# Splitting the products from scores and states around second-layer products in four of seven blocks

## The chip, the cores and the metric

The kernel runs on one core of a Trainium2 chip. The metric is the device time of one execution in microseconds (us), as the median of several runs. The core has TensorE (PE, matrix products; PEld is its loading of weights), VectorE (DVE), ScalarE (ACT), GpSimd (POOL) and SyncE (SP, which issues most DMAs). Each engine works through its own list of instructions in order, and waits for others by semaphores.

## The reference

An attention block of the RWKV-6 kind feeds a two-layer network. There are 4 sequences of 768 tokens, 8 heads of 48 columns; the network has 384 inputs, 2048 hidden columns and 384 outputs, all in 32-bit floats.

```python
for t in range(S):
    cur = np.einsum('bhd,bhe->bhde', u[None] * kt, vt)
    y[:, :, t] = np.einsum('bhd,bhde->bhe', rt, state + cur)
    state = wt[:, :, :, None] * state + np.einsum('bhd,bhe->bhde', kt, vt)
...
h = x @ w_in          # x is y, turned to (tokens, heads * columns)
g = h - np.tanh(h)
out = g @ w_out
```

## The kernel before

**Blocks and units.** The 3072 tokens are taken in 8 blocks of 384 tokens, two for each sequence (`q` is 0 for the first half and 1 for the second). The main loop `for i, blk in enumerate(blocks)` runs the network for block `i`, in 16 units `f`, each of 128 hidden columns. Within it, the attention of the next block (`later`, block `i + 1`) is made bit by bit in the units, so that its result `xT` is ready when block `i + 1` begins. What follows counts blocks by `i`, the block whose network runs; `later.q` is then 1 for even `i` and 0 for odd `i`. Block 7 has no later block, so there are seven phases of each kind.

**A unit.** TensorE first makes the first layer (`first`, line 870: three matmuls into the PSUM tile `hp`, each with 384 columns). ScalarE and VectorE turn `hp` into `g` (lines 873 to 902). Then come the second-layer products that are due: `due` is a list of (time, function, operands), and `add_due(now)` issues those whose time has come, some units after their `g`. In block 0 a unit's second layer is three matmuls of 384 columns (`Second.add`, line 947). In the later blocks a scheme with fewer products is used: VectorE forms sums of pieces of `g` and of the weights (`form_g`, line 917; `form_w`, line 1240), and a unit has six products of 128 columns (`Fewer.add`, line 994), into the PSUM tiles `acc`. A matmul of 32-bit floats stands twice in the profile, each time with a load of weights, so line 870 has six records in a unit, line 947 six, line 994 twelve.

**The attention of the next block.** In chunks of 64 tokens. `own` or `diagonal_in` and `earlier` make the scores within a chunk (tile `scores`, which the code calls `A`; VectorE writes them at lines 396 and 501). `update_1` and `update_2` make the state at each chunk's start: TensorE at line 574, VectorE at line 586 (tiles `states0`, `states1`). The function `plan(i)` has written out by hand in which unit each phase is issued: `results`, the last of them, stands in unit 13 for `i` of 0 and 1 and in unit 12 for the others.

**The results phase.** `Block.together` takes two PSUM tiles (`att0`, `att1`) for the result and adds two products into them for each head and chunk: scores times values, and the decayed `r` (tile `pre`) times the state. All its matmuls stand at line 756. Their operands are small (64 or 48 rows by 48 columns, 64 columns moved). They go in four stretches of 24 products (48 records): scores with `cross` 0, scores with `cross` 1, states with `cross` 0, states with `cross` 1. For a first half of a sequence (`later.q` of 0) the very first chunk has no state, so the states have 80 records instead of 96. Within one `cross` the second stretch adds onto the first, so it begins behind a tiny GpSimd memset (`ended_at`, line 763) that waits for the first stretch's last matmul. After the last stretch, ScalarE copies the result out (`result_out`, line 728, four copies) and SyncE moves the columns that lie elsewhere (`fill_holes`, line 776, six small DMAs).

**Order around it.** In the loop over units the phases other than `results` are issued first, then the DMA loads, then `add_due(now)`, and only then `later.together(ps_a)` (line 1362). So TensorE's list reads: first layer of the unit, second-layer products that are due, scores, states, first layer of the next unit.

Of the kernel before, what the change touches and what calls it, by code (L numbers as in the profile page):

```python
# [63 lines left out]
ALL = tuple(range(NPAIR))  # L64
# [12 lines left out]
UNITS = [(0, 0), (0, 1)] + [u for j in range(NF // 2 - 2) for u in ((1, j), (0, j + 2))] + [(1, NF // 2 - 2),  # L77
                                                                                      (1, NF // 2 - 1)]
LATE = 3

# [43 lines left out]
def kernel(  # L126
# [12 lines left out]
    nc = tc.nc  # L139
# [46 lines left out]
    def draw(names, cols):  # L186
        nc.gpsimd.memset(mask_all[0:L, cols], 1.0)
        for m in names:
# [5 lines left out]
            else:  # L194
# [13 lines left out]
    states = [states0[:, 0:NPAIR * NCH * L].rearrange("d (p c e) -> d p c e", c=NCH, e=L),  # L208
              const.tile([P, NPAIR, NCH, L], F32, name="states1", tag="states1")]
# [13 lines left out]
    def g_at(q, x):  # L223
        if not isinstance(x, str):
# [9 lines left out]
    n_whole = blocks_n * NPAIR * NCH  # L234
    light = [n for n in range(blocks_n * NF) if NF - LATE <= n < blocks_n * NF - 2 and
             (n < NF or few[n // NF])]
# [76 lines left out]
    def begin_behind(ins, then):  # L313
        tc.add_manual_dep(then.ins, ins.ins.name, mybir.DependencyInfo(
            mybir.DependencyClass.Sync, mybir.DependencyReason.DATA))
# [3 lines left out]
    class Block:  # L319
# [408 lines left out]
                    copies.append((copy[h] if copy else nc.scalar.copy)(out=dst[rows], in_=src[rows]))  # L728
            return copies[0]

        def together(self, ps):

            self.results(ps)
            yp, spread, St, ended = self.yp, isinstance(ps, Kept), states[self.q], {}

            def scores(p, c, h, par):
                toks = slice(64 * par, 64 * par + 64)
                return self.v[toks, c, p * D2 + h * D:p * D2 + (h + 1) * D], A[toks, h, p, c, :]

            def from_state(p, c, h, par):  # L740
                rows = slice(64 * h, 64 * h + D)
                return St[rows, p, 2 * c + par, 0:D], self.chunk("pre", p, 2 * c + par, spread)[rows]

            def stretch(of, cross):
                first = cross not in ended
                begun = set()
                for n in range(UP):
                    for c in range(NCP):
                        for h in range(2):
                            for x in range(2):  # L750
                                p, par = UP * n + x, x ^ cross
                                if of is from_state and not (self.q or c or par):
                                    continue
                                lhs, rhs = of(p, c, h, par)
                                e0, n0 = 64 * (h ^ x), (n * NCP + c) * L
                                done = nc.tensor.matmul(yp[x][e0:e0 + D, par, n0:n0 + L], lhsT=lhs, rhs=rhs,  # L756
                                                        start=first and (x, e0) not in begun, stop=True,
                                                        skip_group_check=True)
                                begun.add((x, e0))
                                if not first and len(begun) == 1:  # L760
                                    begin_behind(ended[cross], done)
                if first:
                    ended[cross] = nc.gpsimd.memset(ended_at, 0.0)
                    begin_behind(done, ended[cross])

            for of in (scores, from_state):
                for cross in range(2):
                    stretch(of, cross)
            self.result_out(ALL)
            self.fill_holes([nc.sync])  # L770

        def fill_holes(self, engines, which=range(2 * KC)):
            for n in reversed(which):
# [68 lines left out]
        def general(self, ps):  # L842
            self.begin()
            self.load_v()
            for name, as_ in (("k", "k"), ("r", "r"), ("k", "post"), ("r", "pre")):
                for p0 in HALVES:
                    self.load(name, p0, UP, as_=as_)
            src = wT[self.b, :, :, self.q * NCH * LP:(self.q + 1) * NCH * LP]
            for p in range(NPAIR):
                nc.sync.dma_start(out=self.tokens("w", p, 1).rearrange("d (c t) -> d c t", t=L),  # L850
                                  in_=src[p].rearrange("d (c j) -> d c j", j=LP)[:, :, 1:])
            for name, odd in (("k", 1), ("r", 0)):
                for p in range(NPAIR):
                    t = self.tokens(name, p, 1).rearrange("d (n two) -> d n two", two=2)[:, :, odd]
                    nc.scalar.activation(out=t, in_=t, func=AF.Copy, scale=u_sb[:, p:p + 1])
            for p0 in HALVES:
                mask = masks[1].rearrange("s b j -> s (b j)")
                self.masked(ps, "k", "r", mask, p0)()
                self.decay(1, p0, UP)
                self.totals(1, p0, UP)  # L860
                for m in (2, 4, 8, 16, 32):
                    self.level(ps, m, p0, UP)
                    self.totals(m, p0, UP)
                self.turn(ps, p0)
                self.update_any(ps, p0, self.tots[L])
            self.together(ps)

    def first(xT, f, hp):
        for kc in reversed(range(KC)):
# [336 lines left out]
    ps_a = Kept(mains.enter_context(tc.tile_pool(name="ps_a", bufs=1, space=PSUM)))  # L1206
# [8 lines left out]
    ahead_of_h, rest, formed, extra, behind, due, summed = [], [], [], [], [], [], []  # L1215
# [26 lines left out]
    for i, blk in enumerate(blocks):  # L1242
        here = xT
        later = blocks[i + 1] if i + 1 < len(blocks) else None
# [7 lines left out]
        for f in range(NF):  # L1252
# [36 lines left out]
            rest, behind, formed, forming, held_back = later_ops, [], [], held_back, []  # L1289
# [33 lines left out]
            for of, names in ((later, before.get(f, ())), (after, ahead.get(f, ()) if i else ())):  # L1323
                for name in names if of else ():
                    if not now:
                        late.append(lambda of=of, name=name: of.prepare(name))
                    elif now < 2 or name.startswith("bound"):
                        of.prepare(name)
                if of is later:
                    for name in phases.get(f, ()) if later else ():  # L1330
                        behind += later.phase(ps_a, name)
            if i == 0 and f == NF - 3:
                early.close()
                wide = ctx.enter_context(tc.tile_pool(name="wide", bufs=1))
# [9 lines left out]
            for name in loads.get(f, ()):  # L1344
                of, ins = (after if name in ("w", "k", "r") else later), None
# [13 lines left out]
                    behind.append(summed[0].others_summed)  # L1359
            add_due(now)  # L1360
            if later and "results" in phases.get(f, ()):
                later.together(ps_a)
        if fewer and later:
            summed.append(fewer)
    sum_held(ends[:, 1:3], top[:, n_top - 2:], ends, count)
# [14 lines left out]
    with tc.If(anew > 0, label="anew"):  # L1380
        with tc.manual_schedule(engines={PE, SP, DVE, ACT}), ExitStack() as again_pools:
            ps_d = again_pools.enter_context(tc.tile_pool(name="ps_e", bufs=1, space=PSUM))
            ps_a = again_pools.enter_context(tc.tile_pool(name="ps_b", bufs=2, space=PSUM))
# [64 lines left out]
```

## Time and profile before

| | us |
|---|---|
| median of 3 runs | 552.23 (550.72 to 553.09) |
| the profiled execution | 552.88, its span 551.1 |
| TensorE busy | 536.8 (97% of the span) |
| VectorE busy | 459.3 (83%) |
| ScalarE busy | 403.6 (73%) |
| line 870, first layer, tile hp | 260.1 |
| line 756, the results phases | starting between 78.8 and 466.9 |

In the views, times are from the span's start. A row of the timeline has the start, the length, engine, line, operation, tiles (out<-in), shapes and the number of instructions merged; in square brackets stands the idle time before it and what ended it ("issue" means that the profile shows nothing that the engine waited for). A row of the list of waits has the total, the number of times and the longest. A row of the view by windows has the window and its length, then for PE, PEld, DVE, ACT and POOL the busy time and the number of instructions, then the granted clock of TensorE, the DMA share and GB/s. A row of the DMA queues has packets, MB and share of time.

### The profile page before, as it was taken

The page shows a single profiled execution, that of the slowest core. Times are in us where ns is not written, and L with a number is a line of the kernel's source. Part 1 is how long each engine was busy: PE and PEld are TensorE (multiplying, and loading weights), DVE is VectorE, ACT ScalarE, POOL GpSimd, SP SyncE. Part 2 cuts the span into 40 slices and gives each one's busy share as a digit, 9 for nine tenths or more (in the row PEclk, how much of TensorE's full clock was granted, in tenths as well). Part 3 has the DMA queues.
Part 4 walks back from the last instruction along what each step waited for, and adds up shares of the span by engine and source line. Part 5 has one row for each costly group of instructions (what it writes and reads, how often), then busy time and mean ns, then how long its engine had stood idle before and what let it go on. Part 6 is the DMA issues. An engine that isn't in the chain of part 4 may idle for free.

```text
span 551.1 us, 14091 instructions
## 1 busy us (share of the span) xinstructions
PE 536.8 (97%) x5682; PEld 404.7 (73%) x5682; DVE 459.3 (83%) x943; ACT 403.6 (73%) x814; POOL 6.5 (1%) x47
## 2 busy tenths in 40 slices
PE   8999989999999999999999999999999999999996
PEld 5756655677777787878777787777877777787874
DVE  7899997899979989799897889879787897557563
ACT  5899975897568886688666887588855986666561
POOL 1100000000000000000000000000000000000000
PEclk9999998999999999999999999999999999999999
DMA  7798632252302532144112532126222320200101
GB/s 273 256 398 320 216 116 70 86 129 75 118 11 87 113 113 92 57 122 138 61 55 50 139 117 66 50 87 160 66 86 63 82 63 2 56 0 1 45 1 46
DMA packets 53045, 56.29 MB, mean 102 GB/s; under 512 B 21488, under 2 KB 50928, under 8 KB 52976
## 3 DMA queue, kind: packets, MB, share of 16 engines
q1 hardware_dynamic: 52592, 55.18, 32.8%
q8 instruction: 45, 0.74, 0.6%
q14 instruction: 24, 0.20, 0.1%
q10 hardware_dynamic: 288, 0.10, 0.1%
q0 software_dynamic: 96, 0.07, 0.1%
HBM read 44.73 MB, written 4.72 MB: 90 GB/s over the span
## 4 chain that ended last, share of the span: by engine, by line
PE 92%; DVE 4%; issue 2%; DMA 1%; SPq 0%; DVEq 0%
PE hp L870 43%; PE acc L994 26%; PE att L994 6%; PE acc L947 5%; PE att L756 4%; PE att L493 2%; PE acc L972 2%; PE att L574 2%; PE att L870 1%; DMA r<-in_rT 1%; PE acc L870 1%; DVE scores L501 1%; DVE first_states L630 0%; DVE pre L416 0%; DVE w_sb L267 0%
## 5 line engine op out<-in xcount | busy, mean ns | idle before, releaser
L870 PE MATMUL hp<-xT,w_sb 128*128 128x384 f32 x738 | 260.1, 489 | 0.0
L870 PEld LDWEIGHTS hp<-xT,w_sb 128*128 128x128 f32 x738 | 132.1, 191 | 69.4 <-issue 0.3
L994 PE MATMUL acc<-forms,g 128*128 128x128 f32 x954 | 133.2, 276 | 0.0
L873 ACT ACTIVATE h<-hp 128x384 f32<-128x384 f32 x123 | 60.2, 489 | 98.8 <-PE hp L870 98.3
L994 PEld LDWEIGHTS acc<-forms,g 128*128 128x128 f32 x954 | 122.0, 192 | 10.3
L876 DVE SCALAR_TENSOR_TENSOR h<-h,s 128x384 f32<-128x384 f32 x128 | 70.6, 551 | 60.4 <-ACT s L891 60.4
L917 DVE TENSOR_TENSOR g<-g 128x256 f32<-128x256 f32 x265 | 103.1, 418 | 7.4 <-PE acc L994 6.5
L892 ACT ACTIVATE qa<-s,shift 128x384 f32<-128x384 f32 x113 | 69.5, 615 | 3.7
L894 ACT ACTIVATE junk<-s,shift 128x384 bf16<-128x384 f32 x113 | 67.7, 599 | 0.0
L876 DVE SCALAR_TENSOR_TENSOR g<-qa,h 128x384 f32<-128x384 f32 x112 | 61.5, 550 | 1.6 <-ACT qa L902 0.2
L891 ACT ACTIVATE s<-h 128x384 f32<-128x384 f32 x113 | 59.1, 523 | 3.6
L994 PEld LDWEIGHTS acc<-w_sb,g 128*128 128x128 f32 x318 | 46.8, 191 | 9.7 <-ACT sums L962 0.3
L994 PE MATMUL acc<-w_sb,g 128*128 128x128 f32 x318 | 53.0, 276 | 0.0
L994 PE MATMUL att<-w_sb,g 128*128 128x128 f32 x212 | 35.5, 275 | 0.0
L994 PEld LDWEIGHTS att<-w_sb,g 128*128 128x128 f32 x212 | 31.1, 192 | 5.3
L947 PE MATMUL acc<-w_sb,sums 128*128 128x384 f32 x96 | 34.6, 498 | 0.2 <-DVE sums L876 0.2
L1029 DVE TENSOR_TENSOR sums<-sums 128x256 f32<-128x256 f32 x84 | 32.7, 405 | 1.7 <-ACT sums L1006 1.4
L263 ACT ACTIVATE up<-raw 128x768 f16<-128x768 f32 (+1 forms) x32 | 32.9, 1061 | 0.0
L947 PEld LDWEIGHTS acc<-w_sb,sums 128*128 128x128 f32 x96 | 18.6, 196 | 13.5 <-DVE sums L876 1.1
L416 DVE TENSOR_TENSOR_SCAN pre<-w,start 128x780 f32<-128x780 f32 x14 | 24.9, 1782 | 0.8
L428 DVE TENSOR_TENSOR_SCAN post<-w,seed 128x780 f32<-128x780 f32 x14 | 24.8, 1775 | 0.0
L894 ACT ACTIVATION_READ_ACCUMULATOR junk<-s,shift 128x1 f32 x113 | 21.1, 187 | 0.0
(118 smaller groups left out, 530.1 us busy)
## 6 DMA issues: line engine op xcount, KB each, us to landing
raw<-in_weights SPq DMA_DIRECT2D x16, 768.0 KB, 6.3
w<-in_wT SPq DMA_DIRECT2D x7, 780.0 KB, 4.5
k<-in_kT SPq DMA_DIRECT2D x7, 768.0 KB, 4.7
r<-in_rT SPq DMA_DIRECT2D x7, 768.0 KB, 4.5
v_sb<-in_v SPq DMA_DIRECT2D x8, 576.0 KB, 4.0
k<-in_tokens SPq DMA_DIRECT2D x7, 576.0 KB, 3.9
r<-in_tokens SPq DMA_DIRECT2D x7, 576.0 KB, 4.7
out_y<-sums SPq DMA_DIRECT2D x18, 128.0 KB, 1.8
```

The costliest lines, as they stand in the source:

```text
L263: return lambda: nc.scalar.activation(out=to, in_=of, func=AF.Copy, scale=scale, bias=bias)
L416: return nc.vector.tensor_tensor_scan(out=self.tile("pre")[:, cols], data0=self.tile("w")[:, cols], data1=start[:, 0:n * NCH * LP], initia ...
L870: nc.tensor.matmul(hp, lhsT=w_in_sb[:, f, kc, :], rhs=xT[kc], start=(kc == KC - 1), stop=(kc == 0))
L873: return h, nc.scalar.activation(out=h, in_=hp, func=AF.Copy, scale=1.0 / UPSCALE)
L876: return lambda: nc.vector.scalar_tensor_tensor(out=out, in0=in0, scalar=scalar, in1=in1, op0=op0, op1=ALU.mult)
L891: nc.scalar.activation(out=s, in_=h, func=AF.Square)
L892: nc.scalar.activation(out=qa, in_=s, func=AF.Square, bias=shift[:, 4:5])
L894: nc.scalar.activation(out=junk[:, 0:NB], in_=s, func=AF.Relu, bias=shift[:, 5:6], accum_out=excess[:, at:at + 1])
L917: return lambda: nc.vector.tensor_tensor(out=G[:, to:to + 2], in0=two(G, g_at(q, a0), g_at(q, a1)), in1=two(G, g_at(q, b0), g_at(q, b1)), ...
L947: nc.tensor.matmul(acc, lhsT=g[:, j * P:(j + 1) * P], rhs=w_out_sb[:, f, :], start=(f == self.first), stop=(f == NF - 1))
L994: nc.tensor.matmul(to, lhsT=G[:, g_at(q, a), :], rhs=rhs, start=start, stop=stop, skip_group_check=True)
L1029: ops.append(lambda op=op, at=at: nc.vector.tensor_tensor(out=at[0], in0=at[1], in1=at[2], op=OPS[op]))
```

## The change

`together` becomes `products(ps, part)`, with two parts. Part 0 takes the two PSUM tiles and issues the first two stretches, part 1 issues the other two, the copies and the small DMAs. Which product comes first now depends on the half of the sequence: for `q` of 0 scores come first, as before; for `q` of 1 (even `i`) states come first and scores second.

For `i` of 2, 4 and 6 (`JOINED`) both parts are issued where `together` was, after `add_due`. For `i` of 0, 1, 3 and 5 part 0 is issued with the other phases, ahead of `add_due`, and part 1 behind it, so that TensorE's list reads: first layer, two stretches, second-layer products, two stretches, first layer of the next unit. The GpSimd memsets between a stretch and the one that adds onto it stay, and no drain of TensorE is put in.

```diff
+JOINED = 2, 4, 6
...
-        def together(self, ps):
-
-            self.results(ps)
-            yp, spread, St, ended = self.yp, isinstance(ps, Kept), states[self.q], {}
+        def products(self, ps, part):
+
+            if not part:
+                self.results(ps)
+                self.ended = {}
+            yp, spread, St, ended = self.yp, isinstance(ps, Kept), states[self.q], self.ended
...
-            for of in (scores, from_state):
-                for cross in range(2):
-                    stretch(of, cross)
-            self.result_out(ALL)
-            self.fill_holes([nc.sync])
+            for cross in range(2):
+                stretch((from_state if self.q ^ part else scores), cross)
+            if part:
+                self.result_out(ALL)
+                self.fill_holes([nc.sync])
...
-            self.together(ps)
+            for part in range(2):
+                self.products(ps, part)
...
                     for name in phases.get(f, ()) if later else ():
-                        behind += later.phase(ps_a, name)
+                        if name != "results":
+                            behind += later.phase(ps_a, name)
+                        elif i not in JOINED:
+                            later.products(ps_a, 0)
...
             if later and "results" in phases.get(f, ()):
-                later.together(ps_a)
+                for part in range(i not in JOINED, 2):
+                    later.products(ps_a, part)
```

## The prediction

> **What bounds the kernel now.** I read the page first, then the waits of TensorE alone, then the timeline of TensorE around each of the seven products phases (line 756), then the stretches by window.
>
> ```profile
> span 551.1 us, 14091 instructions
> PE 536.8 (97%) x5682; PEld 404.7 (73%) x5682; DVE 459.3 (83%) x943; ACT 403.6 (73%) x814; POOL 6.5 (1%) x47
> q8 instruction: 45, 0.74, 0.6%
> PE 92%; DVE 4%; issue 2%; DMA 1%; SPq 0%; DVEq 0%
> ```
>
> TensorE is busy 97% of the span and is 92% of the chain that ended last; only its idle time and its slow time can be won. The next answer lists what it waited for between 30 and 540 us, after the start and before the end:
>
> ```profile
> PE att L756 <- issue: 4.8, 4, 1.7
> PE att L756 <- DVE scores L396: 1.4, 1, 1.4
> ```
>
> So 6.2 us stand at line 756 (nothing else there is over 0.2), and two kinds must be told apart: one wait for VectorE, and four that the profile can put down to nobody ("issue"). Block 0 has the first and one of the second:
>
> ```profile
> 72.90 2.10 PE L870 MATMUL hp<-xT,w_sb 128*128 128x384 f32 x6
> 75.19 2.20 PE L947 MATMUL acc<-w_sb,sums 128*128 128x384 f32 x6 [0.19 <-DVE sums L876]
> 78.82 1.56 PE L756 MATMUL att<-scores,v_sb 64*48 64x64 f32 x96 [1.43 <-DVE scores L396]
> 80.20 1.41 PE L756 MATMUL att<-pre,states 48*48 48x64 f32 x85
> 83.26 0.42 PE L756 MATMUL att<-pre,states 48*48 48x64 f32 x11 [1.66 <-issue]
> 83.62 3.11 PE L870 MATMUL hp<-xT,w_sb 128*128 128x384 f32 x6
> 89.28 2.10 PE L870 MATMUL hp<-xT,w_sb 128*128 128x384 f32 x6
> 93.16 2.10 PE L870 MATMUL hp<-xT,w_sb 128*128 128x384 f32 x6
> ```
>
> The other three are in blocks 1, 3 and 5; block 2 shows a phase that has none (4 and 6 look like it):
>
> ```profile
> 145.31 0.61 PE L994 MATMUL acc<-w_sb,g 128*128 128x128 f32 x4
> ...
> 146.74 1.56 PE L756 MATMUL att<-scores,v_sb 64*48 64x64 f32 x96
> 148.12 1.07 PE L756 MATMUL att<-pre,states 48*48 48x64 f32 x57
> 150.26 0.59 PE L756 MATMUL att<-pre,states 48*48 48x64 f32 x23 [1.08 <-issue]
> 150.78 2.20 PE L870 MATMUL hp<-xT,w_sb 128*128 128x384 f32 x6
> ...
> 208.64 1.56 PE L756 MATMUL att<-scores,v_sb 64*48 64x64 f32 x96
> 211.47 2.20 PE L870 MATMUL hp<-xT,w_sb 128*128 128x384 f32 x6
> ...
> 272.60 1.56 PE L756 MATMUL att<-scores,v_sb 64*48 64x64 f32 x96
> 273.98 1.34 PE L756 MATMUL att<-pre,states 48*48 48x64 f32 x70
> 276.03 0.42 PE L756 MATMUL att<-pre,states 48*48 48x64 f32 x10 [0.71 <-issue]
> ...
> 401.47 1.56 PE L756 MATMUL att<-scores,v_sb 64*48 64x64 f32 x96
> 402.85 1.23 PE L756 MATMUL att<-pre,states 48*48 48x64 f32 x65
> 405.43 0.44 PE L756 MATMUL att<-pre,states 48*48 48x64 f32 x15 [1.35 <-issue]
> 405.80 2.20 PE L870 MATMUL hp<-xT,w_sb 128*128 128x384 f32 x6
> ```
>
> The stall falls after 85, 57, 70 and 65 of the second type's matmuls, never at a boundary of the code (a stretch is 48 recorded matmuls, since each product of 32-bit floats is recorded twice). What the four places share is their distance. I counted TensorE's recorded instructions from the middle of each stall to the middle of the next:
>
> ```profile
> 81.90:149.80 67.90, 65.93 (x638) 47.31 (x637) 61.67 (x121) 50.49 (x107) 0.58 (x5) 0.97 0.35 97
> 149.80:275.70 125.90, 125.06 (x1403) 98.51 (x1403) 111.20 (x228) 94.67 (x199) 0.64 (x8) 1.00 0.31 87
> 275.70:404.80 129.10, 128.05 (x1403) 100.71 (x1403) 111.17 (x231) 95.95 (x202) 0.64 (x8) 1.00 0.32 90
> ```
>
> 638 + 637 = 1275 and twice 1403 + 1403 = 2806. The queue named "instruction" carries 0.74 MB in 45 packets, 16.4 KB each, and 11,364 matmuls and weight loads over 45 are 253 a packet. If a packet is 256 instructions, the distances are 5 x 256 = 1280 and 11 x 256 = 2816, less a few synchronising instructions that the rows leave out. So I read the stalls as TensorE running out of fetched instructions: a phase issues a matmul and its load every 14.4 ns (1.38 us for 96), and 192 such pairs are 384 instructions in 2.83 us (208.64 to 211.47). How long a refill needs follows from the rows. In block 1 the stall comes 96 + 57 pairs = 306 instructions into the phase, so the boundary before it was passed after 50, at 147.10; work resumes at 150.26, 3.16 us later. The same working gives 2.9 us in block 3, 3.5 in block 5 and 3.7 in block 0. A block of 256 that is run faster than that ends in a wait.
>
> [...]
>
> The last row of interest is the slow time: line 870 took 3.11 us from 83.62 instead of 2.10.
>
> ```profile
> 77.94:81.35 3.41, 2.53 (x179) 2.53 (x182) 3.41 (x5) 0.85 (x3) 0.18 (x2) 1.00 0.66 226
> 81.35:84.76 3.41, 1.75 (x32) 1.13 (x21) 3.28 (x7) 1.04 (x3) 0.00 (x0) 1.00 0.02 5
> 84.76:88.18 3.42, 3.42 (x7) 1.88 (x6) 3.01 (x6) 1.94 (x5) 0.00 (x0) 0.50 0.12 29
> ```
>
> After a stretch with TensorE busy for only 1.75 of 3.41 us, the granted clock was 0.50 for the next 3.42 us. The stretch before it (2.53 busy) was not followed by a drop.
>
> **The change part by part.**
>
> *Block 0, order.* Now: first layer, six second-layer matmuls (line 947), 96 scores, 96 states. After: first layer, states, the six, scores. The one thing that is late there is VectorE's last write of the diagonal into the scores:
>
> ```profile
> 76.86 1.91 DVE L396 COPY_PREDICATED scores<-mask_all,diagonal 128x768 f32<-128x768 uint8 x2
> ```
>
> The states do not read it, and no wait of TensorE for states or their factors stands in the list. The first layer's follower can start 1.94 us after 72.90, at 74.84 (line 870 repeats every 3.88 us with six others between). Then 1.42 for the states (half of 2.83), 1.94 for the six: 78.20. The scores still wait for that write, which ends at 78.77, so they start at 78.82 as now, and the next first layer at 78.82 + 1.42 = 80.24 instead of 83.62: 3.38 us. This contains the refill: the block of 256 that now ends in the stall then holds 122 small pairs (1.76), the six (1.94) and the wait (0.62), 4.3 us against 3.7 needed, so it no longer starves.
>
> *Block 0, clock.* From 83.62 to 89.28 twelve matmuls take 5.66 us instead of 3.88. With the 1.66 us stall gone I take the halving as gone too: 1.78 us. Bounds: nothing, or 1.78. I take 1.78, because the window from 77.94 would have 0.9 us idle at most, as in the row that caused no drop. [...]
>
> *Blocks 1, 3, 5, order.* Twelve second-layer matmuls (line 994, from 145.31 to 146.74, 1.43 us) go from before the scores to between scores and states. The phases take 4.04 us (146.74 to 150.78), 3.78 (the next line 870 starts 0.35 after 276.03) and 4.33 to the next first layer, against 2.83 x 176 / 192 = 2.60 unstarved: 1.44 + 1.18 + 1.73 = 4.35 us at stake. In the new order the starving block holds 116 small pairs (1.67 us), the twelve (1.43) and about 0.17 of switching: 3.27 us, against 3.16, 2.88 and 3.48 needed. So blocks 1 and 3 just pass, and block 5 is 0.2 short and pays about 0.36 to restart. I take back 0.6 us; the bounds are 0 and, if every refill is as slow as 3.7, 3 x 0.8 = 2.4.
>
> *Switching.* A split adds one turn from large to small matmuls and back. Block 2 shows its price: 192 pairs at 14.4 ns are 2.76 of 2.83 us, and the start comes about 0.1 after the last large one: 0.17 a turn, 0.7 for four blocks.
>
> *Waits.* The second half of each phase waits for a GpSimd memset behind the first half. It is now covered by the other stretch (0.7 us); with the second layer between, by more. No engine gets a wait that it had not. Later second-layer products free their operands later: they end at 273.98 in block 3 instead of 272.5, and VectorE's next write of a form starts after that, with 0.6 of cover:
>
> ```profile
> 274.59 0.42 DVE L917 TENSOR_TENSOR g<-g 128x256 f32<-128x256 f32 x1
> ```
>
> If that cover were gone, VectorE would stand for the overlap, up to 1.4 us, not TensorE at once. ScalarE's four copies, SyncE's six small DMAs and the loads keep their places in their queues; they wait for the phase's end, which comes earlier.
>
> *Blocks 2, 4, 6.* Nothing is split, but states come before scores, so TensorE needs the states 1.42 us sooner:
>
> ```profile
> 206.12 0.36 DVE L586 TENSOR_TENSOR states<-states,whole 128x192 f32<-128x192 f32 x1
> 398.57 0.35 DVE L586 TENSOR_TENSOR states<-states,att 128x192 f32<-128x192 f32 x1
> ```
>
> The last update ends at 206.48, 2.16 us ahead of the phase: cost nothing. In block 5 it ends at 398.92; the scores, which overwrite the PSUM that it reads, would start at 400.04: 1.1 us of cover.
>
> *Does VectorE allow it?* TensorE would be 5.2 us early from block 0 on.
>
> ```profile
> 84.90:111.00 26.10, 26.10 (x91) 16.07 (x91) 20.80 (x37) 18.77 (x43) 0.00 (x0) 0.94 0.27 82
> 111.00:146.70 35.70, 35.70 (x383) 27.79 (x381) 34.84 (x74) 29.44 (x61) 0.41 (x3) 1.00 0.46 123
> ```
>
> VectorE idles 26.10 - 20.80 = 5.3 us up to 111 and then only 0.9 until 146.7. It can come forward by just those 5.3 us, and needs to, since later it has no room. I count this as enough, at its limit.
>
> *Sum.* 3.38 + 1.78 + 4.35 - 0.6 - 0.7 = 8.2 us. The profiled execution took 552.88 us (span 551.1), 0.65 over the median of 552.23; from the median the time is 544.0 us.
>
> **The rivals.**
>
> 1. *Refills still starve the odd blocks.* If the fetch is slower once, or starts later, 1.43 us of cover is too little. If each keeps a stall of 0.6 and a restart of 0.36, 4.35 - 2.9 = 1.5 are left there: 5.16 + 1.5 - 0.7 = 6.0, and 546.2. For it: 3.27 against 3.48 in block 5. Against: blocks 1 and 3.
> 2. *The stall belongs to the states, not to the fetch.* Then it moves with them. In block 0: 74.84 + 1.42 + 1.96 + 1.94 = 80.16, scores end 81.58: 2.0 gained, with the clock 3.8; in the odd blocks 0; less switching 0.7: 550.9, or 549.1 with the clock. Against it: blocks 2, 4 and 6 have the same stretches and no stall. [...]
> 3. *VectorE is the true limit.* It follows only halfway and the odd blocks' gain is lost in the same way: some 2.6 us kept, 549.6. For it: 0.9 us of idle in 35.7. Against: TensorE shows no wait for it there.
> 4. *Slower: the clock gate.* If each half of a split phase counted as idle, up to eight windows would run at half rate, 1.78 us each: 14.2 more, while 8.2 are won: 558. It decides from seven windows. Against it: small matmuls filled most of 2.53 busy us without a drop, and so in all other phases.
>
> **How the numbers follow.** About 0.5% (2.8 us) is what a measurement of this kernel can tell from no change. Forecast 0.72, own range 541.5 to 546; rival 1 0.12; rival 2 0.06; rival 3 0.06; rival 4 0.04. Faster: 0.72 + 0.12 + half of rival 3 = 0.87; slower 0.04; same 0.09. The low end is everything at stake without deductions (9.5, 542.7) less about a microsecond, as the runs spread from 550.72 to 553.09. The high end, 549.0, takes in rival 1 and most of rival 3.
>
> **What would show it.** Right: no "issue" wait over 0.5 us at line 756 in any block; in block 0 scores starting at about 78.8 behind six second-layer matmuls and the next first layer at 80.2; granted clock 1.00 from 84.8; TensorE 5 us earlier at the start of block 1 and still at 146. Wrong: "issue" waits left in blocks 1, 3, 5 (rival 1); a stall inside the states before the second layer (2); new waits of TensorE for VectorE between 100 and 150 us (3); clock below 1.00 in a split phase (4).

## The result, and the profile after

The changed kernel took 545.93 us (545.27 to 548.4, six runs), the kernel before 551.12 (550.69 to 553.09, six runs, among them the three of the table above): a ratio of 0.9904, with a 95% interval from 0.9879 to 0.9928. The forecast was 544.0 us, in a range of 541.5 to 549.0. The profiled executions are 552.88 us before and 546.00 after, which is 6.9 us, while the medians differ by 5.2; the difference between these two numbers is explained below.

From the page after, the span, the busy times and the shares of the chain that ended last, and then TensorE's whole list of waits between 30 and 540 us:

```profile
span 544.3 us, 14092 instructions
PE 535.2 (98%) x5682; PEld 403.6 (74%) x5682; DVE 458.9 (84%) x943; ACT 403.7 (74%) x814; POOL 6.6 (1%) x47
...
PE 93%; DVE 3%; DMA 2%; issue 1%; PEld 0%; SPq 0%; PEldq 0%; DVEq 0%
```

```profile
PE att L759 <- DVE scores L397: 0.3, 1, 0.3
```

The work is the same (5682 matmuls); the four waits with no releaser are gone, and of the wait for VectorE 0.3 of 1.4 us are left. Line numbers are a little higher than before: 756 is 759, 870 is 874, 947 is 951, 994 is 998, 493 is 494. TensorE's timeline in block 0:

```profile
73.41 2.10 PE L874 MATMUL hp<-xT,w_sb 128*128 128x384 f32 x6
75.44 1.56 PE L759 MATMUL att<-pre,states 48*48 48x64 f32 x96
76.94 2.20 PE L951 MATMUL acc<-w_sb,sums 128*128 128x384 f32 x6
79.48 1.56 PE L759 MATMUL att<-scores,v_sb 64*48 64x64 f32 x96 [0.34 <-DVE scores L397]
80.97 2.20 PE L874 MATMUL hp<-xT,w_sb 128*128 128x384 f32 x6
83.00 2.10 PE L951 MATMUL acc<-w_sb,sums 128*128 128x384 f32 x6
84.94 2.10 PE L874 MATMUL hp<-xT,w_sb 128*128 128x384 f32 x6
```

This execution was 0.51 us late when it came here (first layer at 73.41, before at 72.90). The next first layer starts at 80.97 and not at 83.62, and takes 2.20 us and not 3.11. The window in which the clock had been halved now shows 1.00 as the granted clock (third number from the end):

```profile
84.76:88.18 3.42, 3.42 (x13) 1.96 (x12) 3.25 (x7) 1.78 (x6) 0.00 (x0) 1.00 0.32 62
```

Blocks 1 and 5 in TensorE's timeline:

```profile
139.03 2.10 PE L874 MATMUL hp<-xT,w_sb 128*128 128x384 f32 x6
141.06 1.56 PE L759 MATMUL att<-scores,v_sb 64*48 64x64 f32 x96
142.54 0.71 PE L998 MATMUL acc<-w_sb,g 128*128 128x128 f32 x4
143.09 1.06 PE L998 MATMUL acc<-forms,g 128*128 128x128 f32 x8
144.08 1.48 PE L759 MATMUL att<-pre,states 48*48 48x64 f32 x80
145.48 1.24 PE L874 MATMUL hp<-xT,w_sb 128*128 128x384 f32 x3
...
392.13 2.10 PE L874 MATMUL hp<-xT,w_sb 128*128 128x384 f32 x6
394.16 1.56 PE L759 MATMUL att<-scores,v_sb 64*48 64x64 f32 x96
...
397.18 1.80 PE L759 MATMUL att<-pre,states 48*48 48x64 f32 x80
398.91 1.56 PE L874 MATMUL hp<-xT,w_sb 128*128 128x384 f32 x4
```

The states of block 5 take 1.80 us where block 1 needs 1.48: a rest of the wait, 0.33 us, is still there. TensorE's lead over the kernel before, read at the first layer behind each phase, grows at just the four split blocks: 2.65 us behind block 0 (83.62 - 80.97), 4.34 once the slow clock of before is past (89.28 - 84.94), 5.30 behind block 1 (150.78 - 145.48), 5.30 behind block 2 (211.47 - 206.17), 5.98 behind block 3 (276.38 - 270.40) and 6.89 behind block 5 (405.80 - 398.91). With the late start of 0.51 taken out, block 0's order gave 3.16, its clock 1.69, and blocks 1, 3 and 5 gave 0.96, 0.68 and 0.91.

VectorE over the same 36 instructions, before and after (line 876, now 880, stands at both ends; the second window cuts a 37th):

```profile
85.11:111.25 26.14, 26.14 (x93) 16.27 (x92) 20.72 (x36) 18.78 (x42) 0.00 (x0) 0.94 0.27 82
```

```profile
85.67:106.91 21.24, 21.24 (x83) 13.55 (x82) 20.36 (x37) 16.32 (x37) 0.00 (x0) 1.00 0.29 96
```

Before, it idled 26.14 - 20.72 = 5.4 us there; now it idles 21.24 - 20.36 = 0.9. It starts the stretch 0.56 us later than before and ends it 4.34 earlier. It came forward with TensorE and had only just the room for it.

### The profile page after: what moved, and what is told of

It reads as the page before. It is cut to its first block, busy times and chain, and to the rows that moved or that the text cites. A ratio compares the mean times of both kernels' runs of the same rounds, so it can differ in the third digit from the quotient of the medians.

```text
span 544.3 us, 14092 instructions
## 1 busy us (share of the span) xinstructions
PE 535.2 (98%) x5682; PEld 403.6 (74%) x5682; DVE 458.9 (84%) x943; ACT 403.7 (74%) x814; POOL 6.6 (1%) x47
## 4 chain that ended last, share of the span: by engine, by line
PE 93%; DVE 3%; DMA 2%; issue 1%; PEld 0%; SPq 0%; PEldq 0%; DVEq 0%
PE hp L874 43%; PE acc L998 27%; PE att L998 7%; PE acc L951 5%; PE att L759 3%; PE att L494 2%; PE acc L976 2%; PE att L575 2%; PE att L874 1%; DMA xT<-late 1%; DMA r<-in_rT 1%; PE acc L874 1%; DVE scores L502 1%; DVE w_sb L268 0%; DVE post L429 0%
```

## The experiments

Theory A: TensorE's list is fetched in blocks of 256 instructions (the prediction's estimate, from 253 recorded matmuls and loads a packet); a phase that runs a block faster than the next one arrives ends in a wait, and the split helps because slow matmuls then lie in that block. Theory B: the wait belongs to the states' stretch. A third view, called a rival in the expectations: the split as such ends the wait, wherever the fetch stands.

The fetch itself stands in the trace of the kernel before. In the window from 147.5 to 150.2 us, up to the end of block 1's wait, the DMA engines began one packet and nothing else, on the queue named "instruction", at 147.88 us (the sixth of the 40 slices of the first row):

```profile
GB/s 0 0 0 0 0 243 0 0 0 0 0 0 0 0 0 0 0 0 0 0 0 0 0 0 0 0 0 0 0 0 0 0 0 0 0 0 0 0 0 0
q8 instruction: 1, 0.02, 2.2%
```

In blocks 0, 1, 3 and 5 such a packet begins at 80.80, 147.88, 273.58 and 402.49 us, takes 0.9 to 1.4, and TensorE goes on 1.4 to 1.6 us after its end. In block 2, whose phase runs from 208.64 to 211.47 us without a wait, one begins at 205.70 and the next only at 211.11.

The first four kernels below ran on one chip, where the kernel before took 551.75 us (17 runs); the changed kernel with a longer list ran beside the two placed ones, with 552.36 for the kernel before (17 runs); the one with half the work between ran beside the one placed later, with 551.49 (11 runs).

**No block split, order alone.** All blocks joined, so that states come before scores in blocks 0, 2, 4, 6 and nothing else changes.

```diff
-JOINED = 2, 4, 6
+JOINED = 0, 1, 2, 3, 4, 5, 6
```

> The changed kernel with no block split: only the order of the two products is changed in blocks 0, 2, 4 and 6 (states first). Theory A, TensorE runs out of fetched instructions at a fixed place of its list: in block 0 an issue wait of 0.8 to 1.7 us now lies in the scores, which come second; blocks 1, 3, 5 keep 1.1, 0.7 and 1.3 us in the states. Time 549 to 550, against 551.1 for the kernel before. Theory B, the wait belongs to the states: in block 0 it lies in the states, which come first, and the scores have none; time about the same.

Measured: 554.35 us, 1.0048 (1.0029 to 1.0067) of the kernel before. Its profiled execution is the fastest of seven, with 550.98. TensorE in block 0:

```profile
78.11 1.56 PE L759 MATMUL att<-pre,states 48*48 48x64 f32 x96
79.73 1.45 PE L759 MATMUL att<-scores,v_sb 64*48 64x64 f32 x85
83.63 0.42 PE L759 MATMUL att<-scores,v_sb 64*48 64x64 f32 x11 [2.46 <-issue]
83.99 2.20 PE L874 MATMUL hp<-xT,w_sb 128*128 128x384 f32 x6
```

The wait stands in the scores now, after 96 + 85 matmuls as before, so it goes by the place in the list and not by the product: theory B falls here. The time was missed. The wait is longer than expected, 2.46 us, and takes back nearly all that the order gained (from the first layer ahead of the phase, at 73.38, to the one behind it 10.61 us, before 72.90 to 83.62, 10.72). The six other runs took 553.1 to 556.0 us, with a mean granted clock of 0.989 to 0.997 against 1.000 in the profiled one; they left no trace, so that their clock fell in block 0 is only argued. In block 0 the order alone gains next to nothing; the split without the order was not run.

**Block 0 alone.**

```diff
-JOINED = 2, 4, 6
+JOINED = 1, 2, 3, 4, 5, 6
```

> Block 0 split, blocks 1, 3 and 5 joined as before. If the two parts of the gain add up (both theories): block 0's 3.2 us are kept and the 2.6 us of the odd blocks are lost, whose issue waits of 1.1, 0.7 and 1.3 us are back: 547.9, 2.4 to 2.6 over the changed kernel. If VectorE and not TensorE sets the time behind block 0, the waits come back without the time.

Measured: 548.47 us, 0.9935 (0.9915 to 0.9955). Its waits of TensorE:

```profile
PE att L759 <- issue: 3.3, 3, 1.1
PE att L759 <- DVE scores L397: 0.3, 1, 0.3
```

As expected: 2.5 us over the changed kernel's 545.93, which another chip gave, and the three waits are back (1.15, 1.12 and 1.06 us). In the profiles, from the first layer behind block 0's phase to the one behind block 6's it takes 384.6 us against 381.9, 2.7 more. The time comes back with them, so VectorE is not the bound behind block 0.

**All seven split.**

```diff
-JOINED = 2, 4, 6
+JOINED = ()
```

> Blocks 2, 4 and 6 split as well. Theory A: their places in the list cause no wait, so a split gives nothing and costs its two turns between large and small matmuls, 0.30 us each as in the profile of the changed kernel: 0.9 us over the changed kernel, 546.8. A rival, that a split is worth something in itself (cover for the GpSimd memset): 1 us or more under it.

Measured: 546.89 us, 1.0 over the changed kernel's 545.93 from the other chip, without any "issue" wait from 30 us on. From the first layer behind one phase to the one behind the next it is 61.02 us in block 2 (145.00 to 206.02) against 60.69 in the changed kernel (145.48 to 206.17); in blocks 4 and 6 64.30 against 63.96. A split of a phase that has no wait costs 0.34 us and gives nothing. The TensorE rows of block 2, split:

```profile
199.48 2.10 PE L874 MATMUL hp<-xT,w_sb 128*128 128x384 f32 x6
201.51 1.56 PE L759 MATMUL att<-pre,states 48*48 48x64 f32 x96
203.00 1.16 PE L998 MATMUL acc<-forms,g 128*128 128x128 f32 x8
...
204.53 1.56 PE L759 MATMUL att<-scores,v_sb 64*48 64x64 f32 x96
206.02 2.20 PE L874 MATMUL hp<-xT,w_sb 128*128 128x384 f32 x6
```

A stretch of 96 that ends in large matmuls takes 1.49 us to the first of them (201.51 to 203.00), one that is followed by its like 1.38 (78.82 to 80.20 before). What the 0.11 us are, no run shows.

**The kernel before, with a longer list.** 120 instructions more, all in the start.

```diff
-        own = blk.own(ps, h1, spare=94, ahead=5, late=6)
+        own = blk.own(ps, h1, spare=157, ahead=5, late=3)
```

> The kernel before, with TensorE's list made 120 instructions longer during the start (63 more of the small filler matmuls, 3 fewer of the long ones, about 0.3 us in sum), nothing else. Theory A: the issue waits leave blocks 0, 1, 3 and 5 and stand in blocks 2, 4 and 6 instead, 1.1 to 1.7 us each; block 0 keeps its wait of 1.4 us for VectorE; no halved clock from 84 us on; time 549 to 550.5. Theory B: the waits stay in blocks 0, 1, 3 and 5 with their lengths, and the time is 551.4.

Measured: 552.55 us, 1.0016 (0.9995 to 1.0037). Its waits of TensorE, and its timeline in blocks 1 and 2:

```profile
PE att L756 <- issue: 3.5, 3, 1.2
PE att L756 <- DVE scores L396: 1.4, 1, 1.4
```

```profile
146.27 1.56 PE L756 MATMUL att<-scores,v_sb 64*48 64x64 f32 x96
147.65 1.46 PE L756 MATMUL att<-pre,states 48*48 48x64 f32 x80
149.04 2.20 PE L870 MATMUL hp<-xT,w_sb 128*128 128x384 f32 x6
...
206.89 1.56 PE L756 MATMUL att<-scores,v_sb 64*48 64x64 f32 x96
208.27 1.52 PE L756 MATMUL att<-pre,states 48*48 48x64 f32 x92
210.84 0.32 PE L756 MATMUL att<-pre,states 48*48 48x64 f32 x4 [1.05 <-issue]
211.08 2.20 PE L870 MATMUL hp<-xT,w_sb 128*128 128x384 f32 x6
```

The waits changed places as theory A says: 1.05, 1.21 and 1.24 us in blocks 2, 4 and 6, none in 0, 1, 3 and 5; each again ends 1.2 to 1.4 us after an instruction packet has landed. The time was missed by 2 us: the start itself has a dense part, and a refill of 1.31 us now fell there (at 19.3 us), with a halved clock from 21.3 to 24.7. Two numbers are of use later. Block 1's phase, unsplit and unstarved, takes 149.04 - 146.27 = 2.77 us. And block 0, which kept its wait of 1.44 us for VectorE but not the refill, shows no halved clock.

**The changed kernel, with a longer list.** The same edit of the start, made to the changed kernel.

> The changed kernel with the list 120 instructions longer, as in the shifted kernel before. Theory A: the split blocks 0, 1, 3, 5 have no wait wherever the refill falls, the joined blocks 2, 4, 6 now have one each of 1.0 to 1.3 us (with restart 4 to 4.5 in sum), and the start is 1 to 3 us longer as it was there: 550 to 553. So the choice of blocks holds for one length of the list only.

Measured: 551.6 us, 0.9983 (0.9955 to 1.0012). The profile has three "issue" waits at the products' line, 1.16, 1.19 and 1.11 us, all in the joined blocks 2, 4 and 6:

```profile
PE att L759 <- issue: 3.5, 3, 1.2
```

At this length blocks 0, 1, 3 and 5 have no "issue" wait in the kernel before either (the run above), so the run does not test their splits; it shows the joined ones starving. The choice of blocks 2, 4 and 6 holds for one length of the list only: 120 instructions more in the start, and the gain is gone. Of the 5.75 us over the changed kernel beside it (545.85), 4.4 lie in the blocks by the profiles (385.9 us from behind block 0's phase to behind block 6's, against 381.6 in that kernel's profile there), and the rest ahead of them.

**Half the work between.** In blocks 1, 3 and 5 three of the six products go ahead of the scores, three stay between.

```diff
                         elif i not in JOINED:
+                            if i:
+                                _, add, what = due.pop(0)
+                                add(*what, range(3))
+                                due.insert(0, (now, add, (*what, range(3, 6))))
                             later.products(ps_a, 0)
...
-        def add(self, q, part):
+        def add(self, q, part, some=range(6)):
...
-            for n in (FIRST, range(AHEAD_N))[part]:
+            for n in [(FIRST, range(AHEAD_N))[part][k] for k in some]:
```

> The changed kernel, but in blocks 1, 3 and 5 only half of the second-layer products (6 records, 0.7 us) stand between scores and states, the other half ahead of the scores. Theory A: the wait is what a refill needs less what the block of 256 takes, so it goes by the amount of work between: with none it was 1.1 us each, with 12 records 0 to 0.1, here 0.3 to 0.5 us in each of the three blocks; 547 against 545.9. Rival, that a split as such ends the wait (a turn of the array, another order of the semaphores): no wait over 0.1 us, 545.9.

Measured: 547.05 us, 1.7 over the changed kernel's 545.38 on that chip. The states of blocks 1, 3 and 5 in its timeline:

```profile
144.03 1.69 PE L759 MATMUL att<-pre,states 48*48 48x64 f32 x80
...
269.15 1.78 PE L759 MATMUL att<-pre,states 48*48 48x64 f32 x80
...
397.64 1.79 PE L759 MATMUL att<-pre,states 48*48 48x64 f32 x80
```

They take 0.21 to 0.31 us more than the 1.48 of blocks 1 and 3 with twelve records between. The waits are too short to be listed as such (the last matmul's 0.2 us covers them), so they were shorter than the 0.3 to 0.5 expected; but with none, six and twelve records between, the phase lost 1.3 to 1.4 us (block 0 alone split: 4.04 to 4.14 against 2.77 unstarved), 0.2 to 0.3, and 0.0 (but 0.33 in block 5 of the changed kernel's first profile), which is a matter of amount and not of the split as such. In the trace of this kernel the block of 256 took 3.0 to 3.2 us, in that of the kernel with block 0 alone 3.2 to 3.3 with the halt. A refill therefore wants about 3.1 us of work in front of it here; the kernel before's rows gave 2.9 to 3.7. The 0.2 to 0.3 us in three blocks make 0.8. The other 0.9 us of the difference of the medians I can't place; between the two profiles, 1.4 us apart, 0.6 lie ahead of block 0's next first layer (80.92 against 80.34), where the edit changes nothing.

**The list placed instead of split.** Only block 0 split, the list longer by 68 in the start, so that by theory A no refill falls into the dense part of a phase; and nearly the same place (78 instead of 68, counted in blocks of 256) reached with 178 instructions fewer.

```diff
-JOINED = 2, 4, 6
+JOINED = 1, 2, 3, 4, 5, 6
...
-        own = blk.own(ps, h1, spare=94, ahead=5, late=6)
+        own = blk.own(ps, h1, spare=130, ahead=5, late=4)
```

> Only block 0 split, and TensorE's list made 68 instructions longer during the start (36 more short fillers, 2 fewer long ones), so that by theory A no refill falls into the dense part of any phase. Theory A: no issue wait over 0.2 us in any block although blocks 1 to 6 are joined; three splits at 0.30 us and block 5's rest of 0.33 us are saved: 1.2 us under the changed kernel, 544.7, if the start is not longer. Rival, that the split itself is what the odd blocks need: issue waits of about 1.1 us in blocks 1, 3 and 5, 548.5 as with block 0 alone split.

> The same place in the blocks of 256, reached from the other side: the 94 short fillers of the start are left out and 5 more long ones put in, 178 instructions fewer (256 - 178 = 78). The same waits as with 68 more: none over 0.2 us in blocks 1 to 6. The time differs by what the start takes; 544 to 546.

For the second one the fillers are `spare=0, ahead=5, late=11`. The changed kernel ran beside them:

> The changed kernel unedited, for comparison on the chip of the next ones: 545.9, no issue wait over 0.2 us at the products' line.

Measured: 545.83 us placed, 546.86 placed the short way, 545.85 for the changed kernel (0.9871, 0.9834 to 0.9908, of the kernel before there). Placed, TensorE's longest waits from 5 us on are these (two more, of 0.3 and 0.2 us, lie at lines 679 and 697 in the start):

```profile
PE att L494 <- issue: 0.9, 1, 0.9
PE att L494 <- ACT k L454: 0.5, 1, 0.5
PE att L759 <- DVE scores L397: 0.3, 1, 0.3
```

No phase of blocks 1 to 6 waits, though all six are joined, so the rival that the odd blocks need the split falls. From the first layer behind block 0's phase to the one behind block 6's it takes 380.6 us in both (83.42 to 464.01 and 83.11 to 463.70) against 381.9 in the changed kernel's first profile (80.97 to 462.87) and 381.6 in the one beside them, which has no wait left in block 5: of the 1.2 us that were expected 1.0 to 1.3 are there. The medians show nothing of them, so they are lost elsewhere. That it is in the start is argued: the first row above is a wait in the start's own dense part (the short way it is 0.6 us, with 2.1 for ScalarE besides), and the first layer behind block 0's phase comes 2.1 to 2.5 us later than in the changed kernel's first profile. But the changed kernel's profile beside them, with such a wait of 1.5 us, comes there later still, at 84.05.

**Placed later.** Only block 0 split, the start as in the changed kernel, and 64 instructions put into block 0, where TensorE waits for VectorE (0.34 us in the changed kernel).

```diff
-JOINED = 2, 4, 6
+JOINED = 1, 2, 3, 4, 5, 6
...
+                if not i:
+                    passed(hp, 32)
                 for part in range(i not in JOINED, 2):
```

> Only block 0 split, and the list made 64 instructions longer by 32 short fillers into the first layer's PSUM tile in block 0, between its second-layer products and the scores, where TensorE waits 0.3 us for VectorE anyway. The start is left alone. Theory A: no issue wait over 0.3 us in blocks 1 to 6, saved 1.2 us, paid 0.5 us (32 at 27 ns less the wait): 545.2, 0.7 under the changed kernel. If the rest of the wait in block 3 comes back at this length: 545.9.

> The changed kernel once more, on the same chip as the two others: 545.9.

Measured: 546.63 us (545.23 to 548.41) against 545.38 for the changed kernel (545.09 to 545.49; 0.9885, 0.9868 to 0.9903). The fillers took more than the wait gave, and block 3 keeps a short wait:

```profile
78.66 0.95 PE L312 MATMUL hp<-ident 128*16 128x16 bf16 x32
```

```profile
PE att L759 <- issue: 0.2, 1, 0.2
```

In its profile the first layer behind block 6's phase starts at 462.10, in that of the changed kernel on this chip at 461.95. No version was found that beats the changed kernel.

## Why the prediction was right, point by point

*What bounds the kernel, and what the four waits are.* Right, and shown: they move with the length of the list (longer list), stay at their place when the products change places (order alone), shrink with the amount of work in the block (none, half, all), and end 1.2 to 1.6 us after an instruction packet has landed.

*Block 0, order: 3.38 us.* Measured 3.16 between the profiled executions. Of the 0.22 that are missing, 0.15 is the later start of the scores (79.48 - 73.41 = 6.07 us behind the first layer, taken 5.92, of which 0.05 is VectorE's write ending later), and 0.07 the time from there to the next first layer, 1.49 instead of 1.42.

*Block 0, clock: 1.78 us.* Measured 1.69 in the profiled execution. The step failed where it was carried over to the median. The three runs that it was read from (553.09, 550.72, 552.23) were taken as one kind. Of the six runs before, four lie between 550.69 and 551.17; 6.88 us between the profiles less 1.69 is 5.19, and that is the difference of the medians, 551.12 - 545.93 (to the hundredth by chance, since the 6.88 hold the late start of 0.51 too). So most runs of the kernel before seem to go without the drop. That these four had none is argued from the times, but the 45 runs beside the experiments have their mean granted clock on record: in 27 it is 0.998 or more (median 551.4 us), and a halved stretch of 3.41 us takes 0.003 off it (half of 3.41 in 551), so these had none. That the drop went with the halt is not shown: the last section has a longer halt, of 2.46 us, that no drop followed.

*Blocks 1, 3, 5, order: 4.35 at stake, 0.6 taken back.* Measured 2.55 in all (2.9 by the changed kernel's two other profiles, where block 5 has no rest of the wait). Two terms were mis-sized. The unstarved phase was scaled from block 2 by the number of matmuls, 2.60 us; the longer list showed it as 2.77, so at stake were 1.27 + 1.01 + 1.56 = 3.84. And the split costs more, below. The rest in block 5, taken as 0.56 us (0.2 and 0.36 to restart), was 0.33 in one profile and nothing in two; blocks 1 and 3 just pass, as worked out.

*Switching: 0.17 a turn.* The splits of blocks 2, 4 and 6 cost 0.34 us each. The step left out one end of a stretch: the large matmul behind a stretch of 96 starts 1.49 us after its first, a like stretch 1.38 (0.11 of the missing 0.17; the other 0.06 stay open). With 3.84 - 3 x 0.34 - 0.33 = 2.5 us the odd blocks come out.

*Waits, and blocks 2, 4, 6.* Right: no new wait of TensorE stands in the list, and the order in block 2 is free (from behind block 1's phase to behind its own, 60.69 us before and after).

*VectorE.* Right: it followed, at its limit. Rival 3 falls, rival 2 with the order alone, and rival 4 with the clock at 1.00 in every split phase (it is 1.00 from 9.1 to 541.6 us). Rival 1 is seen in small, in block 5.

*The sum, and some luck.* The gain was forecast as 8.2 us and is 5.2, while the time was missed by only 1.9: the 552.23 that the sum was taken from, a median of three runs, lies 1.1 over that of six, and this error worked against the other. Of the 3.0 us, 1.78 are the clock, 0.67 the odd blocks with their splits (3.22 forecast, 2.55 measured), 0.05 block 0 with its split, and 0.51 the late start of the profiled execution, which is no part of the change.

## What to carry to other kernels

A wait of TensorE that the profile puts down to nobody, inside a run of very short matmuls, is to be measured in instructions. Here such waits lay 1275 and 2806 recorded ones apart, which is 5 x 256 and 11 x 256 less 5 and 10, and an instruction packet landed 1.4 to 1.6 us before each ended: signs that the list ran dry. Twelve longer records in the middle ended waits of 1.08 and 0.71 us (blocks 1 and 3), and 120 instructions more ahead moved them all to other blocks. The choice of places made this way held for one length of the list (with those 120 the changed kernel took 551.6 us), so after a later edit that adds instructions look at it again. And before a gain of a slow clock is counted, see in how many runs the clock was slow.

## What was not expected of the hardware

Moving states ahead of scores without a split gave a median slower by 0.5%, though the one profiled execution, at 550.98 us, is not. In it the refill in block 0 came later, 2.46 us of halt instead of 1.66: its packet began, at 81.10, 2.2 us after the place 256 instructions ahead of the halt was passed, against 1.2 in block 0 of the kernel before and 0.4 to 0.9 at its other halts. A load of 768 KB (`k`, 4.5 us) was running then; that it held the packet back is not shown.

How long TensorE is busy in a stretch did not settle here whether the clock fell behind it, as the prediction took it to. These are two stretches of 3.41 us, the length of the halved one in the kernel before, the first from the order alone, the second from the list placed. Like the 81.35 of the kernel before, they begin a whole number of 3.41 us behind the moment at which the clock rose to 1.00 in that execution (6.90, 8.18 and 9.67 us):

```profile
81.99:85.40 3.41, 1.77 (x16) 1.16 (x17) 3.28 (x7) 1.31 (x4) 0.00 (x0) 1.00 0.02 5
```

```profile
18.41:21.83 3.42, 2.48 (x98) 2.04 (x89) 3.24 (x5) 3.42 (x5) 0.58 (x3) 1.00 0.39 71
```

The first, busy for 1.77 us, is followed by a granted clock of 1.00, where the kernel before, busy for 1.75, fell to 0.50. The second, busy for 2.48, is followed by 0.50 for 6.83 us. What counts there stays open.

The start, too, has dense parts with waits that the profile puts down to nobody: in the changed kernel's first profile no such wait over 0.2 us stands at line 494, in its second there is one of 1.5 us:

```profile
PE att L494 <- issue: 1.5, 1, 1.5
```

followed by a granted clock of 0.50 in a window that the first did not have, and 548.72 against 546.00 us:

```profile
22.80:29.60 6.80, 6.56 (x73) 4.41 (x70) 3.53 (x9) 2.69 (x4) 0.00 (x0) 0.50 1.02 368
```

So the same list had the wait in one execution and not in another.
